# Score rows fetched through ScalarE's DMA queue, and the loads of x handed out one by one

## The chip, the cores and the metric

The kernel runs on one core of a Trainium2 chip. The core has five engines that run their own instruction streams and meet through semaphores: TensorE (PE, matmuls into PSUM; its weight loads are shown as PEld), VectorE (DVE), ScalarE (ACT), GpSimd (POOL) and SyncE (SP), which in this kernel only issues DMA transfers. The metric is the device time of one execution in microseconds.

## The reference, cut to what matters

```python
# attention with mixed heads: B=8 batches, H=12 heads, S=448 rows, D=64
scores = scale * q @ k^T                       # per head
scores = einsum('bhij,hg->bgij', scores, w_pre)   # heads mixed before the softmax
attn   = softmax(scores)
attn   = einsum('bhij,hg->bgij', attn, w_post)    # and again after it
x      = (attn @ v) as [B*S, H*D] = [3584, 768]
# dense part
out    = ((x @ w1) * (x @ w2)) @ w3 @ w_out       # 768 -> 1024 -> 1024 -> 768
```

Everything is float32. The weights w3 and w_out are multiplied with each other once, so the dense part is two products in, one product out.

## The kernel before, in words

**Attention.** Heads can only be mixed when the twelve heads of a score row lie on the partition axis. So the scores of a batch are made per pair of heads on TensorE (`qk`, line 175), copied out of PSUM by ScalarE (lines 180 and 181) and stored to DRAM (`raw_d`, lines 186 and 189). From there they are read back in another layout by `fetch` (line 196): ten rows of a batch times twelve heads make a block, two blocks make a **set**, and there are 180 sets. A set's tile `r` has two buffers. Its fetch is two DMAs (line 203), or four where a set crosses the end of a batch (line 210). Then, for set m:

- `mix(m)` on TensorE (line 221) multiplies `r` with w_pre into PSUM banks 2 and 3;
- `largest(m)` on VectorE (line 228) reduces the row minimum (the sign was turned), `exp(m)` on ScalarE (line 236) reads the two banks, so `mix(m+1)` can only start when `exp(m)` has read them;
- `scale(m)` on VectorE and GpSimd (lines 245 to 248) makes the scaled w_post;
- `post(m)` on TensorE (line 261) mixes again, ScalarE copies the result to `mt` (line 275);
- `av` (line 302) multiplies with v, once for fifteen blocks.

**Dense part.** Matmuls are done in three products of split float32 (high and low parts). The first two batches (`ONE = 2`) go one by one with x in SBUF. The other six go in three pairs; a pair's four quarters of x (called 11, 21, 12, 22, three tiles each) are combined in a scheme of seven products instead of eight. Each of the seven products of a layer is a **phase** (`phases`, `layer`): a list of loads (of quarters of x from DRAM), a list of preparations (VectorE sums, a ScalarE cast to the high part at line 641, a GpSimd difference for the low part at line 642) and groups of matmuls (line 703). A phase has 36 matmuls ("atoms"). The loads of a phase are asked for two phases ahead and the preparations are made one phase ahead. The weights of a group, a unit `wu`, are loaded by line 394 into a ring of buffers, three or four units ahead.

**The order of the work** is written out by hand in `run` (from line 891). The loop has 366 steps; set m owns the steps 2m and 2m+1. An even step 2m does: `fetch(m+2)` first (lines 927 and 928); then the stores and loads that the step before put on a list (`do_later`: weight loads, stores, then the loads of x, in this order); `largest(m)`; a share of dense atoms; `exp(m)`; more atoms. An odd step does `scale(m)`, atoms, `av` where it is due, `post(m-1)`, `mix(m+1)`, and the `qk` of later batches with its two copies by ScalarE. Every engine gets its instructions in this order. A wait of one instruction holds up whatever stands behind it on the same engine.

**DMA.** All 1292 transfers are issued by SyncE, in program order. `LATE` (line 34) is step 107, at which buffers of the first phase of the program are given back. `PAIR` is the step at which the pairs begin; `pair_setup` (line 717) issues the first pair's loads of x.

Of the kernel before, what the change touches and what calls it, by code (L numbers as in the profile page):

```python
# [15 lines left out]
B, H, S, D = 8, 12, 448, 64  # L16
# [8 lines left out]
KF, K1 = FF // 128, DM // 128  # L25
IH = IB // 2
HK = H * IH
PP = 64
# [5 lines left out]
LATE = 2 * NB + GB + 2  # L34
# [16 lines left out]
class Kernel:  # L51
# [144 lines left out]
    def fetch(self, m):  # L196
        r = self.rp.tile([128, 2, S], F32, tag="r", name=f"r{m}", bufs=2)
        self.rs[m] = r
        b, t = divmod(2 * m, NB)
        if t + 1 < NB and self.width(2 * m + 1) == IB:  # L200
            src = self.raw_d[b][t * IB:(t + 2) * IB].rearrange("(c s i) h j -> s (i h) c j", c=2, s=2)
            for s in range(2):
                self.nc.sync.dma_start(r[s * PP:s * PP + HK], src[s])
            return
        for c in range(2):
            b, t = divmod(2 * m + c, NB)
            for s in range(2):
                k = self.half(2 * m + c, s)
                src = self.raw_d[b][t * IB + s * IH:t * IB + s * IH + k].rearrange("i h j -> (i h) j")
                self.nc.sync.dma_start(r[s * PP:s * PP + H * k, c], src)  # L210

    def half(self, n, s):
        return min(IH, self.width(n) - s * IH)
# [392 lines left out]
    def layer(self, name, b, nk, pair, groups, h):  # L606

        nc = self.nc
        acc = {g: {} for g in groups}
        ops = {}  # L610
        t2 = [None] * nk
        order, loads = (ORDER3, {}) if b else (ORDER1, {1: (11, 21), 2: (12, 22)})

        def load(q):
            half, batch = q // 20, 2 * pair + (q % 10 == 2)
            assert self.x_made[batch] == 2 * NG
            b[q] = [self.take(f"x{name}_{q}_{k}") for k in range(nk)]
            for k in range(nk):
                nc.sync.dma_start(b[q][k], self.x_d[batch][half][:, k])

        def sub(out, x, y):
            nc.vector.tensor_tensor(out, x, y, op=ALU.subtract)

        def t1(k):
            sub(b[12][k], b[12][k], b[11][k])

        def prepare(m, k):
            x, last = {1: (11, False), 2: (21, False), 3: (22, True), 5: (12, True), 7: (11, True)}.get(m, (0, m == 4))
            x = b[x][k] if x else t2[k]
            if m == 6:  # L630
                x = t2[k] = self.take(f"t{name}_{k}")
                sub(x, b[22][k], b[12][k])
            elif m == 7:
                sub(x, t2[k], x)
            elif m == 4:
                sub(x, b[21][k], x)
                self.give(b[21][k])

            def split():
                hi, lo = (self.take(f"{p}{name}_{m}_{k}", F32R) for p in ("eh", "el"))  # L640
                nc.scalar.copy(hi, x)  # L641
                nc.gpsimd.tensor_tensor(lo, x, hi.bitcast(F32), op=ALU.subtract)  # L642
                ops[m, k] = hi, lo
                if last:
                    self.give(x)

            self.soon.append((None, split))

        def gather(m, g, p):

            a = acc[g]

            def put(out, *to):
                if out not in a:
                    a[out] = self.take(f"c{name}_{g[0]}_{g[1]}_{out}")
                if to:
                    nc.vector.tensor_tensor(a[out], a[to[0]], p, op=ALU.add)  # L657
                else:
                    nc.scalar.copy(a[out], p)

            if m == 1:
                put(11 if order == ORDER3 else 12)
            elif m == 2:
                put(11, 11 if order == ORDER3 else 12)
                ready(g, 11)
            elif m == 6:
                put(12, 11 if order == ORDER3 else 12)
            elif m == 7:
                put(21, 12)
            elif m == 5:  # L670
                put(22, 21)
                put(12, 12)
                ready(g, 22)
            else:
                q = {3: 12, 4: 21}[m]
                put(q, q)
                ready(g, q)

        def ready(g, q):
            f, w = g  # L680
            if w == 1:
                def mult():
                    x, y = acc[f, 0][q], acc[f, 1][q]
                    nc.gpsimd.tensor_tensor(x, x, y, op=ALU.mult)
                    self.give(y)
                    h[q][f] = x
                self.soon.append((None, mult))
            elif w == 3:
                d, batch = f + (q // 20) * K1 // 2, 2 * pair + (q % 10 == 2)
                dst, x = self.out[d * 128:(d + 1) * 128, batch * S:(batch + 1) * S], acc[g][q]  # L690

                def store():
                    nc.sync.dma_start(dst, x)
                    self.give(x)
                self.later.append(store)

        def group(m, g):
            w = self.next_unit()
            i = self.next_bank()
            p = self.bank(i, f"e{name}_{m}_{g[0]}_{g[1]}")[:, :S]  # L700
            for k in range(nk):
                for t, (x, y) in enumerate(PAIRS):
                    nc.tensor.matmul(p, w[:, k, x], ops[m, k][y],  # L703
                                     start=(k == 0 and t == 0), stop=(k == nk - 1 and t == 2))
                    yield
            if g == groups[-1]:
                for k in range(nk):
                    self.give(*ops.pop((m, k)))
            self.ends.append((i, lambda: gather(m, g, p)))

        early = order[order.index(6) - 1]
        for m in order:
            jobs = [lambda k=k: t1(k) for k in range(nk)] if m == early else []
            yield ([lambda q=q: load(q) for q in loads.get(m, ())],
                   [lambda k=k, m=m: prepare(m, k) for k in range(nk)] + jobs, [group(m, g) for g in groups])

    def pair_setup(self, phases):
# [7 lines left out]
    def pair_experts(self, phases):  # L725

        for i, (_, _, groups) in enumerate(phases):
            todo = [f for x in phases[i + 2:i + 3] for f in x[0]]
            todo = [lambda f=f: self.x_due.append(f) for f in todo]
            todo += [f for x in phases[i + 1:i + 2] for f in x[1]]  # L730
            n, each = 0, min(6, 30 // len(todo)) if todo else 1
            for g in groups:
                for _ in g:
                    if n % each == 0 and todo:
                        todo.pop(0)()
                    n += 1
                    yield
            assert not todo
# [315 lines left out]
```

## Time and profile before

| | |
|---|---|
| median of three runs | 1438.72 us (1436.74 to 1440.12) |
| profiled execution, its own time | 1439.32 us |
| its span, first to last instruction | 1437.5 us, mean granted TensorE clock 0.989 |
| busy: PE / PEld / DVE / ACT / POOL | 1382.0 / 1053.5 / 741.6 / 832.5 / 619.8 us |
| DMA moved | 416.87 MB, 290 GB/s on average |

How to read it. A matmul's start is measured and its end is modelled; neighbouring matmuls overlap, so a row's duration is longer than the distance to the next one. An idle time is put down to what ended it. A DMA-issuing instruction is not counted as busy; on the timeline it has the time that its engine's sequencer needed to issue it, and its transfer lands some microseconds later. "SPq" is SyncE's sequencer. Times on the timeline are from the start of the span; set 54, the first that the change touches, is mixed at about 394 us, and the last set at about 1241 us. After that only the dense part of the last pair remains.

### The profile page before, as it was taken

The page shows a single profiled execution, that of the slowest core. Times are in us where ns is not written, and L with a number is a line of the kernel's source. Part 1 is how long each engine was busy: PE and PEld are TensorE (multiplying, and loading weights), DVE is VectorE, ACT ScalarE, POOL GpSimd, SP SyncE. Part 2 cuts the span into 40 slices and gives each one's busy share as a digit, 9 for nine tenths or more (in the row PEclk, how much of TensorE's full clock was granted, in tenths as well). Part 3 has the DMA queues.
Part 4 walks back from the last instruction along what each step waited for, and adds up shares of the span by engine and source line. Part 5 has one row for each costly group of instructions (what it writes and reads, how often), then busy time and mean ns, then how long its engine had stood idle before and what let it go on. Part 6 is the DMA issues. An engine that isn't in the chain of part 4 may idle for free.

```text
span 1437.5 us, 45779 instructions
## 1 busy us (share of the span) xinstructions
PE 1382.0 (96%) x18684; PEld 1053.5 (73%) x18684; DVE 741.6 (52%) x1497; ACT 832.5 (58%) x1952; POOL 619.8 (43%) x754
## 2 busy tenths in 40 slices
PE   5779999999999999999999999999999999999998
PEld 2357786776677667776777777777777777899988
DVE  6867567667544545432444436333445446345563
ACT  4867666777766656665656557556555445432231
POOL 2433233434433544532345336334335446446693
PEclk8989999999999999999999999999999999999999
DMA  9998789999989999999989978799879757698775
GB/s 294 368 330 274 241 271 314 318 312 312 330 281 348 350 363 318 373 357 338 289 268 295 320 259 280 249 318 350 285 223 297 239 176 224 195 337 270 230 232 172
DMA packets 203761, 416.87 MB, mean 290 GB/s; under 512 B 20528, under 2 KB 120112, under 8 KB 203472
## 3 DMA queue, kind: packets, MB, share of 16 engines
q1 hardware_dynamic: 203552, 413.94, 87.4%
q8 instruction: 149, 2.44, 0.7%
q14 instruction: 60, 0.49, 0.1%
HBM read 279.77 MB, written 134.09 MB: 288 GB/s over the span
## 4 chain that ended last, share of the span: by engine, by line
PE 80%; DMA 11%; DVE 4%; ACT 2%; issue 1%; POOL 1%; SPq 0%; DVEq 0%; POOLq 0%; ACTq 0%
PE e L703 20%; PE psa L302 11%; PE pso L261 10%; PE psm L221 8%; PE psq L175 7%; PE eg L523 5%; PE psf L361 4%; PE eo L554 4%; PE e2o L703 4%; PE e3o L703 4%; PE e1o L703 3%; DMA wu<-w_d 3%; DMA raw_d<-st 2%; DMA r<-raw_d 2%; DMA x<-x_d 1%
## 5 line engine op out<-in xcount | busy, mean ns | idle before, releaser
L248 POOL TENSOR_SCALAR w<-wpo,ri 128x60 f32<-128x60 f32 x360 | 180.4, 517 | 487.1 <-DVE ri L246 467.8
L228 DVE TENSOR_REDUCE mn<-psm 128x1 f32<-128x448 f32 x360 | 207.6, 618 | 322.5 <-PE psm L221 322.2
L275 ACT COPY mt<-pso 128x480 f32<-128x480 f32 x352 | 197.9, 621 | 184.5 <-PE pso L261 184.3
L703 PE MATMUL e<-eh,wu 128*128 128x448 f32 x1008 | 296.7, 371 | 5.3 <-DVE c L657 3.2
L236 ACT ACTIVATE e<-psm,mn 128x448 f32<-128x448 f32 x360 | 226.8, 642 | 7.9 <-DVE mn L228 7.9
L703 PEld LDWEIGHTS e<-eh,wu 128*128 128x128 f32 x1008 | 187.5, 188 | 50.9 <-issue 25.7
L221 PE MATMUL psm<-r,wsc 60*64 60x448 f32 (+1 forms) x1440 | 194.0, 552 | 21.1 <-DVE cx L125 8.3
L261 PEld LDWEIGHTS pso<-w,e 60*64 60x64 f32 x10080 | 174.7, 134 | 50.7 <-issue 42.5
L261 PE MATMUL pso<-w,e 60*64 60x60 f32 x10080 | 198.5, 224 | 0.4 <-ACT mt L275 0.3
L703 PE MATMUL e<-el,wu 128*128 128x448 f32 x504 | 186.9, 371 | 0.0
L302 PE MATMUL psa<-mt,v 128*64 128x150 f32 (+1 forms) x2304 | 156.9, 292 | 3.2 <-ACT st L180 3.2
L175 PE MATMUL psq<-kq 64*64 64x448 f32 x1176 | 156.4, 542 | 3.4 <-ACT st L180 3.4
L302 PEld LDWEIGHTS psa<-mt,v 128*64 128x64 f32 x2304 | 143.6, 137 | 19.3 <-ACT st L180 5.9
L657 DVE TENSOR_TENSOR c<-c,e 128x448 f32<-128x448 f32 x168 | 101.6, 617 | 87.5 <-PE e L703 82.9
L180 ACT COPY st<-psq 128x448 f32<-128x448 f32 x162 | 86.4, 533 | 77.1 <-ACT mt L275 33.5
L523 PE MATMUL eg<-xh,wu 128*128 128x448 f32 x384 | 119.1, 380 | 4.8 <-DMA wu<-w_d 4.8
L642 POOL TENSOR_TENSOR el<-x,eh 128x448 fp32r<-128x448 f32 x90 | 103.8, 1173 | 31.8 <-ACT eh L641 26.2
L703 PEld LDWEIGHTS e<-el,wu 128*128 128x128 f32 x504 | 94.6, 188 | 22.6 <-issue 14.1
L175 PEld LDWEIGHTS psq<-kq 64*64 64x64 f32 x1176 | 61.2, 135 | 57.7 <-issue 29.7
L523 PEld LDWEIGHTS eg<-xh,wu 128*128 128x128 f32 x384 | 71.4, 189 | 37.5 <-issue 24.0
L245 DVE TENSOR_SCALAR sa<-sm 128x2 f32<-128x2 f32 x180 | 35.5, 197 | 115.1 <-ACT e L236 114.6
L181 ACT COPY st<-psq 128x448 f32<-128x448 f32 x162 | 87.6, 541 | 0.0
(99 smaller groups left out, 2007.5 us busy)
## 6 DMA issues: line engine op xcount, KB each, us to landing
r<-raw_d SPq DMA_DIRECT2D x344, 210.0 KB, 5.0
raw_d<-st SPq DMA_DIRECT2D x138, 448.0 KB, 5.7
wu<-w_d SPq DMA_DIRECT2D x104, 384.0 KB, 6.6
wu<-s_d SPq DMA_DIRECT2D x96, 384.0 KB, 4.9
wu<-w_d SPq DMA_DIRECT2D x51, 512.0 KB, 5.7
kq<-kq SPq DMA_DIRECT2D x42, 448.0 KB, 7.4
wu<-s_d SPq DMA_DIRECT2D x36, 512.0 KB, 5.1
x<-x_d SPq DMA_DIRECT2D x72, 224.0 KB, 5.8
```

The lines of the kernel that those rows point to most:

```text
L175: nc.tensor.matmul(ps[s][z * PP:(z + 1) * PP], t[rows, q:q + PP], t[rows, k:k + S], start=True, stop=True)
L221: nc.tensor.matmul(ps[s][c * PP:(c + 1) * PP, :S], self.wsc[k], r[k, c], start=True, stop=True)
L228: self.nc.vector.tensor_reduce(mn[:, s:s + 1], self.psm[m][s][:, :S], axis=AX.X, op=ALU.min)
L236: nc.scalar.activation(e, p[:, :S], AF.Exp, bias=mn[:, s:s + 1], scale=-1.0, accum_out=sm[:, s:s + 1])
L248: nc.gpsimd.tensor_scalar_mul(w2[:, s], self.wpo, ri[:, s:s + 1])
L261: nc.tensor.matmul(self.pso[c][z * PP:(z + 1) * PP, at:at + HK], e[k, j * PP:(j + 1) * PP], w2s[k, s], start=True, stop=True)
L275: self.nc.scalar.copy(dst.rearrange("p j g (s i) -> p j s g i", s=2), src)
L302: nc.tensor.matmul(self.psa[rows, g % 3, :W], v[:, j, rows], mt[:, j, 2 * g + s, :W], start=(j == 0), stop=(j == NJ - 1))
L523: nc.tensor.matmul(p, u[:, k % (K1 // 2), x], xs[y][:, k], start=(k == 0 and t == 0), stop=(k == K1 - 1 and t == 2))
L642: nc.gpsimd.tensor_tensor(lo, x, hi.bitcast(F32), op=ALU.subtract)
L657: nc.vector.tensor_tensor(a[out], a[to[0]], p, op=ALU.add)
L703: nc.tensor.matmul(p, w[:, k, x], ops[m, k][y], start=(k == 0 and t == 0), stop=(k == nk - 1 and t == 2))
```

## The change

Two edits. In `fetch`, the DMAs of sets whose first block has a number of at least 107 (sets 54 to 179) are issued by ScalarE instead of SyncE, at the same place of the program order: at the head of the even step, ahead of the step's other instructions. ScalarE has a DMA queue of its own. In the pairs, a load of a quarter of x, until now one job that issues its three tiles, becomes three jobs of one tile each. These jobs alternate with the preparations of the phase, a preparation first, and are called every three atoms; before, the two quarters' jobs came first, at atoms 0 and 6, and the preparations followed every six atoms. This touches ten phases, those two phases ahead of a layer's first and second product; the loads that `pair_setup` issues stay as they are.

```diff
     def fetch(self, m):
...
+        dma = self.nc.scalar.dma_start if 2 * m >= LATE else self.nc.sync.dma_start
...
-                self.nc.sync.dma_start(r[s * PP:s * PP + HK], src[s])
+                dma(r[s * PP:s * PP + HK], src[s])
...
-                self.nc.sync.dma_start(r[s * PP:s * PP + H * k, c], src)
+                dma(r[s * PP:s * PP + H * k, c], src)
...
-        def load(q):
+        def load(q, only=None):
...
-            b[q] = [self.take(f"x{name}_{q}_{k}") for k in range(nk)]
-            for k in range(nk):
+            b[q] = b.get(q, [None] * nk)
+            for k in range(nk) if only is None else (only,):
+                b[q][k] = self.take(f"x{name}_{q}_{k}")
                 nc.sync.dma_start(b[q][k], self.x_d[batch][half][:, k])
...
-            yield ([lambda q=q: load(q) for q in loads.get(m, ())],
+            yield ([lambda only=None, q=q: load(q, only) for q in loads.get(m, ())],
...
-            todo = [f for x in phases[i + 2:i + 3] for f in x[0]]
-            todo = [lambda f=f: self.x_due.append(f) for f in todo]
-            todo += [f for x in phases[i + 1:i + 2] for f in x[1]]
-            n, each = 0, min(6, 30 // len(todo)) if todo else 1
+            loads = [f for x in phases[i + 2:i + 3] for f in x[0]]
+            loads = [lambda f=f, k=k: self.x_due.append(lambda: f(k)) for f in loads for k in range(K1 // 2)]
+            made = [f for x in phases[i + 1:i + 2] for f in x[1]]
+            todo = [f for x in itertools.zip_longest(made, loads) for f in x if f]
+            n, each = 0, min(6, max(30, 3 * K1 // 2 * len(groups) - 16) // len(todo)) if todo else 1
```

## The prediction

> **What bounds the kernel now.** I read the head of the page, then TensorE's waits from 380 us on, where the changed part begins, then SyncE's waits, the table by stage, and last the timelines of the places where TensorE stood still.
>
> ```profile
> span 1437.5 us, 45779 instructions
> ...
> PE 1382.0 (96%) x18684; PEld 1053.5 (73%) x18684; DVE 741.6 (52%) x1497; ACT 832.5 (58%) x1952; POOL 619.8 (43%) x754
> ```
>
> ```profile
> PE eg L523 <- DMA wu<-w_d: 4.8, 4, 1.8
> PE psm L221 <- DMA r<-raw_d: 3.4, 2, 2.0
> ...
> PE e L703 <- DMA wu<-w_d: 1.4, 1, 1.4
> ```
>
> TensorE is the bound. From 380 us on it waits for transfers seven times, 9.6 us in all: that is the most the change can win, 0.7%. These waits have their place, as three stages of the table by stage show (the columns are the stretch and its length, the granted clock, the DMA engines' busy share, GB/s):
>
> ```profile
> 475.00:530.00 55.00, 0.94 1.03 364
> 960.00:1010.00 50.00, 1.00 1.04 348
> 700.00:760.00 60.00, 1.00 0.81 253
> ```
>
> The first two hold most of the waits, and there all sixteen DMA engines are full (share 1.0); the third is a quiet stage with 0.81. In full stages a transfer is late because the DMA engines are behind, whoever issues it.
>
> SyncE's own longest wait is the fetch, which stands at the head of the even step and cannot start before the mix that last read its buffer:
>
> ```profile
> SPq L203 <- PE psm L221: 243.4, 81, 6.2
> ```
>
> So in quiet stages the fetch holds up what is queued behind it on SyncE, 3.0 us at a time (243.4 / 81). In the full stages something else holds it. The chain of waits there, and SyncE's queue in order:
>
> ```profile
> 986.43 7.07 DMA x<-x_d
> ...
> 993.57 6.28 DMA r<-raw_d
> ```
>
> ```profile
> 986.43 2.62 SPq L619 DMA_DIRECT2D x<-x_d  x3
> 989.75 0.32 SPq L394 DMA_DIRECT2D wu<-w_d  x1
> 990.23 0.34 SPq L693 DMA_DIRECT2D out<-c1o  x1
> 991.16 2.19 SPq L619 DMA_DIRECT2D x<-x_d  x3
> 993.57 0.88 SPq L203 DMA_DIRECT2D r<-raw_d  x2
> ```
>
> The fetch at 993.57 is issued when the x load of 986.43 has landed (986.43 + 7.07 = 993.50), and that load stands eight places ahead of it: 3 + 1 + 1 + 3. Eight transfers are in flight and the ninth waits for the oldest. I take it that this count goes by program order over both queues. **This is the point on which the forecast rests:** then a fetch on ScalarE waits for the same old transfer, and ScalarE stands still meanwhile, where until now only SyncE did.
>
> **The fetch, part by part.** Removed from SyncE and added to ScalarE: sets 54 to 179, 120 with two DMAs and 6 with four, 264 issues.
>
> ```profile
> L203 SPq DMA_DIRECT2D r<-raw_d x344: 315/392/1914, 14.9 to 1224.7; - x172
> ```
>
> ```profile
> L236 ACT ACTIVATE e<-psm,mn 128x448 f32<-128x448 f32 x256 | 161.6, 644 | 5.0 <-DVE mn L228 5.0
> L275 ACT COPY mt<-pso 128x480 f32<-128x480 f32 x251 | 141.1, 621 | 160.2 <-PE pso L261 160.1
> ```
>
> ```profile
> 988.59 0.54 ACT L181 COPY st<-psq 128x448 f32<-128x448 f32 x1
> 989.01 0.58 ACT L641 CAST eh<-x 128x448 fp32r<-128x448 f32 x1
> 989.48 0.65 ACT L236 ACTIVATE e<-psm,mn 128x448 f32<-128x448 f32 x1
> ```
>
> At the median of 0.392 us on SyncE that is 103 us of ScalarE's sequencer, 0.8 us per set in front of `exp`. ScalarE's instructions overlap (the cast starts 0.12 us before the copy has ended), so its sequencer runs ahead of the engine, and the two copies of `st` that stand before the fetch can cover the issue. Bounds: 0 (all covered) to 0.8 us per set. I take it as covered: even uncovered it ends in ScalarE's 160 us of waiting for `post`. Without that cover it lands on `exp`, and behind `exp` on the next mix, which needs the banks that `exp` reads; that is a rival below.
>
> **The new wait.** Queued behind a waiting fetch are the casts of the step, `exp`, then the copies; TensorE's next mix waits for `exp`. For each late fetch: how far its end lies behind the start of the first ScalarE instruction after it; that delay moves the end of `exp` (two of 0.644, so 1.28 after its start); what lies beyond the start of the next mix is a stall.
>
> ```profile
> 473.69 1.15 ACT L484 CAST s<-y 128x512 fp32r<-128x512 f32 x2
> 475.16 0.66 ACT L236 ACTIVATE e<-psm,mn 128x448 f32<-128x448 f32 x1
> 475.45 0.88 SPq L203 DMA_DIRECT2D r<-raw_d  x2
> 476.61 0.54 PE L221 MATMUL psm<-r,wsc 60*64 60x448 f32 x1
> ...
> 513.74 0.52 ACT L484 CAST s<-y 128x384 fp32r<-128x384 f32 x1
> 514.22 0.64 ACT L236 ACTIVATE e<-psm,mn 128x448 f32<-128x448 f32 x1
> 516.84 1.18 SPq L203 DMA_DIRECT2D r<-raw_d  x2
> 517.14 0.54 PE L221 MATMUL psm<-r,wsc 60*64 60x448 f32 x1
> ...
> 586.20 0.65 ACT L236 ACTIVATE e<-psm,mn 128x448 f32<-128x448 f32 x1
> 586.77 1.19 SPq L203 DMA_DIRECT2D r<-raw_d  x2
> 588.48 0.54 PE L221 MATMUL psm<-r,wsc 60*64 60x448 f32 x1
> ...
> 663.24 1.84 ACT L641 CAST eh<-x 128x448 fp32r<-128x448 f32 x3
> 664.99 0.63 ACT L236 ACTIVATE e<-psm,mn 128x448 f32<-128x448 f32 x1
> 666.96 1.55 SPq L203 DMA_DIRECT2D r<-raw_d  x2
> 665.93 0.54 PE L221 MATMUL psm<-r,wsc 60*64 60x448 f32 x1
> ...
> 992.32 0.54 PE L221 MATMUL psm<-r,wsc 60*64 60x448 f32 x1
> ```
>
> - At 475: fetch ends 476.33, delay 2.64, `exp` ends 476.44 + 2.64 = 479.08, mix at 476.61: 2.5. SyncE may have come late here for reasons of its own, so 2.0.
> - At 517: fetch ends 518.02, delay 4.28, `exp` 515.50 + 4.28 = 519.78, mix at 517.14: 2.6.
> - At 587: fetch ends 587.96; a cast of about 0.4 stands between; `exp` from 588.4 to 589.7, mix at 588.48: 1.2.
> - At 667: fetch ends 668.51, delay 5.27, `exp` 666.27 + 5.27 = 671.54, mix at 665.93: 5.6. Its two issues took 1.55 against a median of 0.78; with that 0.77 off, 4.8.
> - At 993: fetch ends 994.45, delay 5.44, `exp` 990.76 + 5.44 = 996.20, mix at 992.32: 3.9.
>
> Together 14.5 us. A neighbouring late fetch adds nothing: TensorE then stands still while the DMA engines catch up. For the same reason the old waits in these places go: 4.8 for weights and 3.4 for r, 8.2. The net is +6.3. Bounds: half the new wait, if fewer transfers are in the way, 7.2 - 8.2 = -1.0; nothing replaced, +14.5.
>
> **What SyncE gains.** The 243 us of waiting no longer stand in front of weights and loads. I take 0: these waits end in quiet stages, where TensorE does not wait for transfers. Bounds: 0 to the 1.4 us of `wu` at 1100 that the sum has not used.
>
> **The loads of x.** Sixty tile loads in ten phases stay on SyncE, same issues, later by up to 24 - 6 = 18 atoms; of six, one comes in the first step of the phase, then two, then three, so they still come bunched. The DMA engines have the same bytes to move in the full stage around 990: 0. Preparations come 12 atoms earlier and have a phase of room before the matmuls read them: 0. The first load now has 33 atoms until its cast:
>
> ```profile
> 727.36 3.85 PE e L703 x18
> ```
>
> ```profile
> DMA to landing us min/median/max: 4.6/5.8/8.6
> ```
>
> 33 x 3.85 / 18 = 7.1 us of dense matmuls alone, with attention in between, against 8.6 at worst for landing (the view of line 619). Bounds: 0 to about 1.5 us each for the few that fall in a full stage, +3; I take 0.
>
> **Sum.** The profiled execution took 1439.3 us, 1.8 more than its span and 0.6 more than the median of 1438.7. 1439.3 + 6.3 - 0.6 = **1445 us**.
>
> The Trainium skill has two rules that bear on this. "DMA: Bandwidth & Descriptors", section "Issuing engines are not separate DMA queues": transfers from several issuing engines share the same sixteen DMA engines, and a second issuer only saves issue time; the full stages here agree (share 1.03 and 1.04), and by it the fetch lands no sooner. The same page, "Queues, rings and completion order": each DMA engine takes turns between the queues that have work, packet by packet; by it the fetch would pass what is queued on SyncE's ring. No run here has two queues yet, and the sum above is the same by both, since the wait lies before the issue.
>
> **Rivals.**
>
> - *SyncE's freedom wins.* With no fetch in front, weights go out 3 us sooner before each full stage, the eight places are free when ScalarE comes, and the old waits go: 9.6 us at most, so 1429; with half the r waits left, about 1432. For it: the 243.4 us. Against: the full stages are 35 to 55 us long, and nothing can be moved out of them by 3 us. By the skill's rule of shared engines the r waits of 3.4 stay and it would be 1438.7 - 6.2 = 1432.5; by the rule of taking turns they go and it is 1429.
> - *The two cancel.* The fetches are themselves among the eight and land sooner on a ring of their own, so that ScalarE waits half as long: 7.2 new against 8.2 old, 1438.
> - *Issue on ScalarE costs more.* If it is not covered, or takes longer than on SyncE, it decides where `exp` ends less than 0.8 us before the next mix, which is before about 690 us (at 475 above: 476.44 against 476.61). Forty-odd sets at 0.2 more each: 9 us on top, 1454.
>
> **How the numbers follow.** The forecast has 0.47 with its own range 1442 to 1450; costly issue 0.12; cancelling 0.21; freedom 0.20. What this kernel's measurement can tell from no change is about 0.2%, 2.9 us. Slower: 0.47 + 0.12, less a little of the forecast's low end, 0.57; the same 0.23; faster 0.20. The range 1432 to 1454 leaves about a tenth out on each side.
>
> **What would show it.** In ScalarE's sequencer waits of the fetch by DMAs, several us long near 475, 517, 667 and 990; in TensorE's waits a line of `psm` on ScalarE's `e` of some 10 to 15 us from 380 us on, and those on `r` and `wu` smaller. SyncE's wait at line 203 for `psm` falls to the first 53 sets. If `psm` on `e` stays below 3 us, my reading of the eight places is wrong; if it is spread over many sets, it is the issue time.

## The result, and the profile after

The changed kernel takes 1452.04 us (median of six runs, 1446.64 to 1456.34) against 1440.36 us for the kernel before on the same chip (1436.74 to 1442.04, six runs). The ratio is 1.0088, with a 95% interval of 1.0066 to 1.011. So it is 11.7 us slower, where 6.3 were forecast. Run again beside other kernels it took 1449.3 us against 1439.2, a ratio of 1.0082 (1.0052 to 1.0111). The profiled execution took 1446.7 us, span 1445.0, which is 7.4 us over the profiled one of before. It was one of the two fastest of the six. The new lines of the kernel shift its line numbers by one from line 199 on, and by two behind the load of x.

The head of the page after, and its queues (packets, megabytes, share of the sixteen engines' time):

```profile
span 1445.0 us, 45817 instructions
...
PE 1387.5 (96%) x18684; PEld 1055.8 (73%) x18684; DVE 745.3 (52%) x1497; ACT 840.0 (58%) x1952; POOL 624.7 (43%) x754
...
q1 hardware_dynamic: 169514, 359.99, 73.5%
q10 hardware_dynamic: 34038, 53.95, 13.1%
```

Queue q10 is ScalarE's and new; it carries the fetches. TensorE does the same matmuls and is still the bound. Its waits after, from 380 us on, all of them (total, times, longest):

```profile
PE psm L222 <- ACT e L237: 13.0, 11, 3.0
PE e L705 <- DVE c L659: 2.6, 3, 1.5
PE e L705 <- ACT eos L562: 0.9, 1, 0.9
PE e L705 <- ACT c L661: 0.2, 1, 0.2
```

The names: `psm` is the mix, `e` in front of L237 the result of `exp`; `eos` and `c` are ScalarE's and VectorE's copies and sums of the dense part's results, `eg` (below) its matmuls in the first two batches. One of the eleven waits of `psm` for `e`, 0.44 us at 380 us, lies ahead of the first fetch on ScalarE (387.7 us), and the kernel before has it as well, at 378.9 us (from its waits between 370 and 385 us):

```profile
PE psm L221 <- ACT e L236: 0.4, 1, 0.4
```

Apart from that one there were, before, 9.6 us of waits for weights and for r, and none of `psm` for `e`. After, every wait for a transfer is gone, and 12.5 us of the mix waiting for `exp`, in ten places, have come. In sum TensorE waits 16.3 us in place of 13.4.

The largest of these stalls shows how it comes about. First TensorE, then ScalarE with its queue, then SyncE's queue; each row has its start, its length, and in brackets the idle time before it with what ended it:

```profile
521.22 1.08 PE L262 MATMUL pso<-w,e 60*64 60x60 f32 x56
525.28 2.38 PE L222 MATMUL psm<-r,wsc 60*64 60x448 f32 x8 [2.98 <-ACT e L237]
```

```profile
518.15 1.14 ACT L276 COPY mt<-pso 128x480 f32<-128x480 f32 x2
521.94 2.06 ACTq L204 DMA_DIRECT2D r<-raw_d  x2
524.09 0.51 ACT L485 CAST s<-y 128x384 fp32r<-128x384 f32 x1 [4.81 <-DMA raw_d<-st]
524.51 0.63 ACT L237 ACTIVATE e<-psm,mn 128x448 f32<-128x448 f32 x1
```

```profile
516.36 1.30 SPq L186 DMA_DIRECT2D raw_d<-st  x2
518.58 0.33 SPq L395 DMA_DIRECT2D wu<-w_d  x1
520.03 0.33 SPq L488 DMA_DIRECT2D s_d<-s  x1
522.42 0.32 SPq L395 DMA_DIRECT2D wu<-w_d  x1
523.16 0.32 SPq L488 DMA_DIRECT2D s_d<-s  x1
523.58 0.37 SPq L395 DMA_DIRECT2D wu<-w_d  x1
```

ScalarE's two fetch issues take 2.06 us, because the second waits. What ends the wait is a store of raw scores, which has nothing to do with these rows: it writes another batch. Counted back in program order over both queues it stands eight places ahead: two stores, `wu`, `s_d`, `wu`, `s_d`, `wu`, and the set's own first fetch. By the trace's DMA records that store landed at 523.65 us, and the second fetch was issued at 523.67. The first fetch had waited too: the transfer eight places ahead of it, the second one of the set before, landed at 521.84 us, and it was issued at 521.94. The records also show what the eight are. The transfers of both queues tell of their landing through the same eight semaphores (100 to 104 and 106 to 108), handed out in turn; the store and the second fetch both have 106. ScalarE did nothing for 4.81 us, `exp` began at 524.51, and the mix behind it stood for 2.98 us. In the whole trace at least 18 of the 264 fetch issues (of some predecessors the landing is not recorded) were made within 0.1 us of the landing of the transfer eight places ahead, at 431 to 496, 524 to 541, 620 to 691, 786 to 792, 1005 and 1102 to 1107 us.

The waits do not show the whole price. The groups of the two matmul lines that use ScalarE's results, from 380 us on, before and after:

```profile
L221 PE MATMUL psm<-r,wsc 60*64 60x448 f32 x1030 | 130.3, 544 | 3.5 <-DMA r<-raw_d 3.4
L175 PE MATMUL psq<-kq 64*64 64x448 f32 x776 | 98.1, 535 | 0.0
```

```profile
L222 PE MATMUL psm<-r,wsc 60*64 60x448 f32 (+1 forms) x1032 | 136.2, 545 | 13.0 <-ACT e L237 13.0
L175 PE MATMUL psq<-kq 64*64 64x448 f32 x776 | 102.4, 539 | 0.0
```

The busy time of the mix has grown by 5.9 us and that of `psq` by 4.3, with the same instructions. A mix writes two banks. When the first `exp` has freed its bank, TensorE starts, and then stands again until the second `exp`, 0.6 us later, frees the other. That second stop lies between matmuls of one group, where ends are modelled, so the trace counts it as busy. It shows in the starts: in the set that stalls at 1007.8 us the first and the last of the eight matmuls start 1.1 us apart, in an undisturbed set (two are shown below) 0.4 to 0.5.

```profile
L222 PE MATMUL psm<-r,wsc x8: 536/562/587, 1007.8 to 1008.9; 60*64 60x448 f32 x8
```

In all ten sets with a stall the distance is larger, in nine by that 0.6 us and in one, at half clock, by 1.0. The `psq` that follow begin within the same stop, so the 5.9 and the 4.3 us are in part the same time.

With two issues a set, the issue itself costs nothing that shows. On ScalarE one takes less than on SyncE (0.392 us before):

```profile
L204 ACTq DMA_DIRECT2D r<-raw_d x240: 322/323/1856, 387.7 to 1232.4; - x120
```

And through the quiet stage the two kernels keep step. The mixes of sets 120 and 140 (eight matmuls each; shortest, median and longest in ns, start of the first and of the last), before and after:

```profile
L221 PE MATMUL psm<-r,wsc x8: 536/539/542, 837.9 to 838.4; 60*64 60x448 f32 x8
...
L221 PE MATMUL psm<-r,wsc x8: 536/539/542, 980.0 to 980.4; 60*64 60x448 f32 x8
```

```profile
L222 PE MATMUL psm<-r,wsc x8: 536/539/542, 844.8 to 845.2; 60*64 60x448 f32 x8
...
L222 PE MATMUL psm<-r,wsc x8: 536/539/542, 987.1 to 987.5; 60*64 60x448 f32 x8
```

That is 142.1 us for twenty sets before and 142.3 after. By the starts of the mixes, the changed kernel falls back in the full stages: by 2.3 us between sets 60 and 72, 5.7 between 80 and 96 and 1.1 between 140 and 144. Between 96 and 112 it makes up 2.4.

### The profile page after: what moved, and what is told of

It is laid out like the page before. It is cut to its first block, busy times and chain, and to the rows that moved or that the text cites. A ratio compares the mean times of both kernels' runs of the same rounds, so it can differ in the third digit from the quotient of the medians.

```text
span 1445.0 us, 45817 instructions
## 1 busy us (share of the span) xinstructions
PE 1387.5 (96%) x18684; PEld 1055.8 (73%) x18684; DVE 745.3 (52%) x1497; ACT 840.0 (58%) x1952; POOL 624.7 (43%) x754
## 4 chain that ended last, share of the span: by engine, by line
PE 47%; DMA 4%; DVE 1%; ACT 1%; issue 0%; ACTq 0%; POOL 0%; SPq 0%; DVEq 0%; POOLq 0%
PE e L705 20%; PE psa L303 5%; PE pso L262 5%; PE psm L222 4%; PE e2o L705 4%; PE e3o L705 4%; PE e1o L705 3%; DMA x<-x_d 2%; PE psq L175 2%; DMA wu<-w_d 1%; ACT e L237 0%; DMA v<-v 0%; DMA r<-raw_d 0%; DVE c L659 0%; DVE c L624 0%
## 5 line engine op out<-in xcount | busy, mean ns | idle before, releaser
L237 ACT ACTIVATE e<-psm,mn 128x448 f32<-128x448 f32 x360 | 225.2, 633 | 46.0 <-DVE mn L229 9.8
L222 PE MATMUL psm<-r,wsc 60*64 60x448 f32 (+1 forms) x1440 | 198.2, 552 | 30.1 <-ACT e L237 19.8
L175 PE MATMUL psq<-kq 64*64 64x448 f32 x1176 | 159.8, 541 | 4.7 <-ACT st L180 4.7
```

Source lines behind the costliest of these rows:

```text
L175: nc.tensor.matmul(ps[s][z * PP:(z + 1) * PP], t[rows, q:q + PP], t[rows, k:k + S], start=True, stop=True)
L222: nc.tensor.matmul(ps[s][c * PP:(c + 1) * PP, :S], self.wsc[k], r[k, c], start=True, stop=True)
L237: nc.scalar.activation(e, p[:, :S], AF.Exp, bias=mn[:, s:s + 1], scale=-1.0, accum_out=sm[:, s:s + 1])
```

## The experiments

Theory: a fetch on ScalarE waits for the transfer eight places ahead and holds `exp`, and with it the mix. Rivals: the loads of x; the issue itself; the second queue; SyncE's order.

**Half of the change: the fetch alone**

```diff
+        dma = self.nc.scalar.dma_start if 2 * m >= LATE else self.nc.sync.dma_start
...
-                self.nc.sync.dma_start(r[s * PP:s * PP + HK], src[s])
+                dma(r[s * PP:s * PP + HK], src[s])
...
-                self.nc.sync.dma_start(r[s * PP:s * PP + H * k, c], src)
+                dma(r[s * PP:s * PP + H * k, c], src)
```

> Half of the change alone: ScalarE issues the score rows from set 54 on, the pairs' loads of x stay as before in jobs of three tiles. Theory (a fetch that waits for an old transfer holds up exp, and exp the next mix): nearly the whole loss is here, 6 to 12 us above the kernel before, and TensorE's wait of psm for e from 380 us on is again 10 to 15 us (13.0 with both halves). Rival (the spread loads of x cost half of it, through ScalarE's 16.7 us of waiting for x): no more than half, 3 to 6 us above.

Measured: 1454.47 us (1449.82 to 1461.73), ratio 1.011 (1.0077 to 1.0143), 14.6 us slower. The whole loss is here, and more than the range I gave. `psm` on `e` was 7.0 us only, below the 10 to 15 expected; other instructions of ScalarE were held in its place:

```profile
775.05 1.05 ACTq L211 DMA_DIRECT2D r<-raw_d  x2
775.43 0.54 ACT L181 COPY st<-psq 128x448 f32<-128x448 f32 x1
776.40 2.52 ACTq L211 DMA_DIRECT2D r<-raw_d  x2
778.96 0.56 ACT L642 CAST eh<-t 128x448 fp32r<-128x448 f32 x1 [2.99 <-DMA wu<-w_d]
```

This is set 112, whose rows lie in two batches and need four transfers. The last two issues waited for a weight load, and behind them stood a cast that TensorE then waited for (1.62 us at 778). The prediction had counted six such sets, and gave them no cost of their own.

**The other half: the loads of x alone**

```diff
-        dma = self.nc.scalar.dma_start if 2 * m >= LATE else self.nc.sync.dma_start
+        dma = self.nc.sync.dma_start
```

> The other half alone: the pairs' loads of x go out one tile at a time between preparations, the score rows stay with SyncE. Theory: within 2 us of the kernel before, up to 2 us slower, psm never waits for e longer than 1 us in all beyond the kernel before. Rival (the spread loads are half of the loss): 4 to 6 us slower, with casts that wait for x.

Measured: 1437.04 us (twelve runs, 1433.95 to 1441.68) against 1439.87 (23 runs), ratio 0.9978 (0.9961 to 0.9994). Neither the theory nor the rival: it is 2.8 us faster, little more than can be told from no change. TensorE's first three waits, from 380 us on:

```profile
PE eg L524 <- DMA wu<-w_d: 3.4, 3, 2.1
PE e L705 <- DVE c L659: 3.2, 5, 1.5
PE psm L222 <- DMA r<-raw_d: 2.3, 1, 2.3
```

The wait for r of 1.5 us at 998 us, which was in the profile of before, is not there. SyncE's queue at that place now has the x loads in ones and twos between weights and stores, so fewer of them stand right ahead of a fetch. One profile of each doesn't show that this is the whole gain. ScalarE's casts did wait for x here, 13.9 us in all (0.7 before, 16.7 in the changed kernel), and it cost nothing that the time shows. So these waits alone aren't the loss.

**The fetch on ScalarE, but behind exp**

```diff
-            if not odd and LF <= n + LF < N:
+            if not odd and LF <= n + LF < N and n + LF < LATE:
                 self.fetch(m + LF // 2)
...
             if not odd and m < SETS:
                 self.exp(m)
+            if not odd and LATE <= n + LF < N:
+                self.fetch(m + LF // 2)
```

> The changed kernel, but from set 54 on ScalarE issues the fetch after the two exp of the even step instead of ahead of them; queue, count and addresses as in the changed kernel. Theory (the wait in front of exp is the loss): psm's wait for e from 380 us on falls from 13.0 to under 4 us, the time falls by 4 to 9 us against the changed kernel, to 1443 to 1448; something of it comes back as waits for r, since the rows are asked for half a step later. Rival (ScalarE's issue time, or the second queue's use of the DMA engines, is the loss wherever the issue stands): within 2 us of the changed kernel's 1452.

Measured: 1444.56 us (twelve runs, 1436.88 to 1450.92), ratio 1.0032 (1.0011 to 1.0053). That is 7.5 us less than the changed kernel's 1452.04, and 4.7 less than the 1449.3 of its later runs. From the waits, 380 us on, of an execution of 1446.86 us:

```profile
PE psm L222 <- DMA r<-raw_d: 3.7, 6, 1.3
PE e L705 <- ACT eos L562: 3.4, 1, 3.4
...
PE psm L222 <- ACT e L237: 0.4, 1, 0.4
```

Queue, count and bytes are the same. What stands behind a waiting fetch has changed, and with the fetch's place in the program order also which transfer is eight ahead of it. ScalarE still stands behind fetches, for up to 4.6 us, but now in front of the copies `mt` and `eos`. `psm` on `e` falls from 13.0 to 0.4 us, as the theory says, and those 0.4 us lie at 380 us, ahead of the change. So more than half of the loss is not the second queue's. A loss of some 4.7 us is left; in the profile the copies `eos` and `c` are now late (3.4 and 2.4 us), and the rows come a little late.

**SyncE's fetch behind the step's other transfers**, the same edit in the kernel before:

```diff
-            if not odd and LF <= n + LF < N:
+            if not odd and LF <= n + LF < N and n + LF < LATE:
                 self.fetch(m + LF // 2)
...
             if not odd and m < SETS:
                 self.exp(m)
+            if not odd and LATE <= n + LF < N:
+                self.fetch(m + LF // 2)
```

> The kernel before, but from set 54 on SyncE issues the fetch later in the even step, behind the step's stores, weights and loads of x, so that it no longer stands in front of them; ScalarE issues nothing. Theory (SyncE's 243 us of waiting for psm hide in quiet stages and are worth nothing): within 3 us of the kernel before, with more waiting for r in the full stages and less for weights. Rival (SyncE's freedom is worth something, and the change only lost it again on ScalarE): 3 to 8 us faster than before.

Measured: 1455.23 us, ratio 1.0111 (1.0074 to 1.0147). 15.4 us slower, though ScalarE issues nothing; neither the theory nor the rival had that. TensorE's wait for r and SyncE's longest wait:

```profile
PE psm L221 <- DMA r<-raw_d: 10.7, 7, 3.3
```

```profile
SPq L189 <- ACT st L181: 152.6, 59, 4.6
```

SyncE's wait of 243.4 us for `psm` is not saved. Most of it moves to the stores, which wait for ScalarE's copies (17.8 us before), and the fetch then stands behind these and comes late. So in this kernel, on SyncE, its place at the head of the step is worth 15 us.

**Twice as many issues on ScalarE**

```diff
             for s in range(2):
-                dma(r[s * PP:s * PP + HK], src[s])
+                for i in range(2 if 2 * m >= LATE else 1):
+                    p = slice(30 * i, 30 * i + 30) if 2 * m >= LATE else slice(0, HK)
+                    dma(r[s * PP + p.start:s * PP + p.stop], src[s][p])
```

> The changed kernel, but each of ScalarE's two fetch transfers of a set is issued as two of half the rows: four issues a set instead of two, the same bytes, the same place. Theory (the fetch waits for the transfer eight places ahead, in the full stages): the third and fourth issue wait for younger transfers, so psm's wait for e from 380 us on grows from 13 to 20 us or more, all of it in the full stages at 430 to 690 and near 1000 and 1100, and the time by 5 to 20 us over the changed kernel. Rival (the issue itself costs ScalarE): 126 sets at 2 more issues of 0.32 us, some 80 us if they are not covered, spread over all stages, the quiet ones between sets 112 and 140 too.

Measured: 1524.08 us (four runs), ratio 1.0582 (1.0541 to 1.0623), 72 us over the changed kernel. That is far over the 5 to 20 that the theory gave, and near the rival's 80. The profiled execution was the slowest of the four (1534.13).

```profile
PE psm L224 <- ACT e L239: 38.6, 20, 5.7
```

```profile
r<-raw_d ACTq DMA_DIRECT2D x498, 105.0 KB, 4.4
```

The transfers, now half as large, are no slower (4.4 us to landing, 4.8 in the changed kernel). In the quiet stage between sets 118 and 136 a set takes 0.24 us more than before (128.75 against 124.37 us for 18). Over all 126 sets that would be some 31 us: an estimate of the part that doesn't depend on the stage. It need not be issue time alone, since ScalarE stands behind a waiting fetch there too, once for 2.4 us. The rest stands in the full stages: the lag behind the kernel before grows by 23 us between sets 56 and 72, by 27 between 80 and 96, and by 13 between 136 and 144. So both have a share once a set has four issues, and the one in the full stages is the larger.

**ScalarE's fetch only from the pairs on**

```diff
-        dma = self.nc.scalar.dma_start if 2 * m >= LATE else self.nc.sync.dma_start
+        dma = self.nc.scalar.dma_start if 2 * m >= 4 * NB + 11 else self.nc.sync.dma_start
```

> The changed kernel, but ScalarE issues the fetch only from the pairs on (set 96 and after); before that SyncE does. Theory: the loss goes with the full stages, of which all but those near 1000 and 1100 lie before the pairs: 1439 to 1444, psm's wait for e at most 5 us from 380 us on. Rival (every fetch on ScalarE costs the same): two thirds of the 126 sets remain, so two thirds of the loss, about 1448.

Measured: 1447.96 us (1446.47 to 1456.34), ratio 1.0077 (1.0047 to 1.0107). I had the place wrong: the time is the rival's, and `psm` waits 8.7 us for `e`, not at most 5. But the loss isn't paid evenly, as the rival has it. Of the 7 us that the profile lies behind from set 88 to the end, five come between sets 88 and 96, where the pairs begin and their loads of x go out together, and none between sets 120 and 140; three more come up to set 112, and one is made up at the end. The place:

```profile
668.00 1.01 ACTq L204 DMA_DIRECT2D r<-raw_d  x2
669.13 1.50 ACT L643 CAST eh<-x 128x448 fp32r<-128x448 f32 x3 [3.84 <-DMA x<-x_d]
670.53 0.62 ACT L237 ACTIVATE e<-psm,mn 128x448 f32<-128x448 f32 x1
```

```profile
671.30 1.21 PE L222 MATMUL psm<-r,wsc 60*64 60x448 f32 x5 [3.21 <-ACT e L237]
```

Three casts stand between the late fetch and `exp` and add 1.4 us to its delay.

**The fetch on GpSimd**

```diff
-        dma = self.nc.scalar.dma_start if 2 * m >= LATE else self.nc.sync.dma_start
+        dma = self.nc.gpsimd.dma_start if 2 * m >= LATE else self.nc.sync.dma_start
```

> The changed kernel, but GpSimd issues the fetch from set 54 on, at the same place in the order; loads of x spread as in the changed kernel. Theory (what costs is that ScalarE stands in front of exp while the fetch waits): psm's wait for e is under 2 us from 380 us on; GpSimd stands still instead, whose products of the weights w2 and whose el come later. If its waits are as long as ScalarE's and its work has room, the time is that of the spread loads alone, 1435 to 1442; if TensorE then waits for w2 or el as it did for e, 1445 to 1455. Rival (a second queue beside SyncE's slows the transfers whoever issues it): 1448 to 1456, with waits for wu or r.

Measured: 1437.52 us (twelve runs), ratio 0.9994 (0.9975 to 1.0013): as the loads of x alone (1437.04). TensorE's wait of `psm` for `e`, what GpSimd does for its fetches, and SyncE's longest wait:

```profile
PE psm L222 <- ACT e L237: 0.9, 1, 0.9
```

```profile
L204 POOL DMA_DIRECT2D r<-raw_d x240: 634/666/900, 385.5 to 1223.6; - x120
```

```profile
SPq L189 <- ACT st L181: 187.3, 63, 5.4
```

Here SyncE is as free of the fetch as in the changed kernel, ScalarE never stands behind a fetch, and nothing is won. The mix and `psq` are back at 129.9 and 98.8 us. Two things changed at once: the engine that stands is another, and by the DMA records GpSimd's transfers use eight semaphores of their own (111 to 118), so its fetches aren't among the eight. This run alone doesn't part the two. The one with the fetch behind `exp` does so for more than half of the loss: there the two queues shared the eight as in the changed kernel.

**The changed kernel once more**

> The changed kernel once more, beside the others on this chip. Expected 1450 to 1454 as a median. Theory on the clock: TensorE runs at a granted clock of 0.5 for some 3 or 7 us behind a pause of two microseconds or more, so an execution with two or three such pauses in the changed part is 2 to 7 us longer than its waits say. Rival: the spread between executions has nothing to do with the pauses, and the stretches of low clock stand elsewhere.

Measured: 1449.3 us (1445.69 to 1455.91), a little below the 1450 to 1454 expected; profiled span 1447.2 us, `psm` on `e` 11.0 us. Its two stretches of low clock stand behind pauses of 2.2 us at 521 and 2.0 at 672, as the theory on the clock has it (a third pause, 1.7 us at 1008, has none behind it), and the last section shows more; how much of the spread between executions it makes remains open.

## Why the prediction was right, and where its sizes were off

**The point on which the forecast rested** held: eight transfers in flight, counted in program order over both queues, and a fetch on ScalarE that stands until the eighth ahead has landed. The 0.02 us between landing and issue shows it, and moving the fetch behind `exp` shows that more than half of the loss arises there.

**The new wait**, 14.5 us in five places, was 12.5 in ten. But the sum counted each stall to the end of the second `exp`, and the profile's wait ends with the first. With the second stop of 0.6 us for each set, the stalls are 2.0 us at 475 (given as 2.0), 1.5 and 3.6 at 517 (2.6), 1.5 at 593 (1.2 at 587), 2.7 at 674 (4.8 at 667) and 2.5 at 1006 (3.9 at 993). The two that were given as largest were little more than half of that. A neighbouring late fetch was to add nothing, and at 517 two sets in a row stalled. Stalls of 0.8 to 1.6 us at 434, 623, 781 and 1098 us were not foreseen.

**The old waits** were to fall by 8.2; all 9.6 went, and with them some 2.4 us of second stops behind late rows in the kernel before (sets 69, 96 to 99 and 143).

**The terms that were mis-sized** are these two: the stalls, 18.6 us in place of 14.5, and what they replace, 12.0 in place of 8.2. The net by this count is +6.6 against the +6.3 of the sum, because the two errors cancel; that is luck. Between the two profiles 6.0 of the 7.4 us come after 380 us; 1.4 had come before the first changed instruction. In these 6.0 us TensorE's waits account for 16.3 - 13.4 = 2.9, and 3.1 are growth of its busy time, in which the second stops lie. The clock works against them: the kernel before has a stretch of half clock (last section) that took 3.4 us of full clock, the changed kernel's took 1.7, which is also why `eg` fell from 66.9 to 64.7 us. These parts don't add up closer than to a microsecond or two. The distance from 7.4 to the median's 11.7 lies between executions: the profiled one had a granted clock of 0.990, the five others 0.982 to 0.986. That clock doesn't order them strictly (1446.64 us at 0.985), so where these 4.3 us come from stays open.

**Issue time, taken as covered,** was: nothing in the quiet stage. The rival that made it 9 us falls. What neither had is the sets with four transfers. In the fetch alone set 112 paid, and not because an issue is long: the last two of the four waited for a weight load. That four take half of the eight places is the likely reason; no run varies it by itself.

**The rival that the two cancel** falls as well. The fetches land hardly sooner on their own queue (median 4.8 us, before 4.9 over the same stretch), and the new waits are 12.5, not 7.2.

**SyncE's freedom, taken as 0,** was 0 within what the runs can tell, and the rival falls: with GpSimd as the issuer SyncE is free, nobody pays for it, and the time is that of the loads of x alone. The Trainium skill, "DMA: Bandwidth & Descriptors", section "Issuing engines are not separate DMA queues", says that a second issuer saves only the time to initiate a transfer. These runs agree (1437.5 us with GpSimd, 1437.0 without a second issuer). They show besides that the new issuer pays for the waiting: ScalarE stood 4.81 us behind the fetch of one set.

**The loads of x, taken as 0 with a bound of +3,** were -2.8 (ratio 0.9978). The sign of the bound was wrong; that spread loads leave fewer transfers ahead of a fetch is the likely reason. That the two edits together lie 2.4 us (1452.04) below the fetch alone (1454.47) fits, but those intervals overlap.

The fastest kernel of the study is the loads of x alone, 1437.0 us. It lies below both the kernel before and the changed one, and level with the fetch on GpSimd.

## What to carry to other kernels

A transfer moved to a compute engine takes its waits with it. Before moving one, count which transfer it will wait for, and read what stands behind it on the new engine in the place where the DMA engines are full, before what its issue takes. If it must move, put it behind the instruction that others wait for, or on an engine that has room, as GpSimd had here. And one that the next step needs early belongs at the head of its queue: SyncE's long wait there was not a cost.

## What the hardware showed that was not expected

**Short pauses of TensorE are often followed by a stretch at half its clock.** The granted clock is the share of TensorE's full clock that the chip gave it. The columns are the stretch and its length, busy times and counts of PE, PEld, DVE, ACT and POOL, granted clock, DMA share, GB/s. The kernel before, behind a pause of 1.75 us for weights:

```profile
521.03 0.47 PE L523 MATMUL eg<-xh,wu 128*128 128x448 f32 x1 [1.75 <-DMA wu<-w_d]
```

```profile
522.00:529.00 7.00, 6.06 (x73) 3.95 (x75) 2.09 (x4) 1.12 (x2) 2.73 (x3) 0.52 1.04 374
```

In these seven microseconds 7 x (1 - 0.52) = 3.4 us of full clock are lost, nearly twice the pause. The changed kernel, behind a pause of 2.06 us at 673.80, loses nothing:

```profile
676.00:683.00 7.00, 7.00 (x99) 4.50 (x100) 2.62 (x8) 4.66 (x12) 3.29 (x6) 1.00 1.05 378
```

In all ten profiles, from 380 us to the last matmul, every stretch of low clock stood at or right behind a pause or a pair of pauses of 1.6 to 5.8 us in all, and took away 1.7 or 3.4 us of full clock, in one place 5.1. Of the pauses in that range some were followed by none, such as the 3.21 us at 668 us in the run with ScalarE's fetch from the pairs on. The Trainium skill, "TensorE: Matmul & The Clock Gate", section "HAM oscillation — how this bites in real kernels", puts the rule at no idle gaps over about 3.4 us. Here 1.75 us was enough in one execution, and 3.21 not in another, so the rows don't bear out a fixed length of that size. With the clock that goes with it, a pause can so cost 1.4 to three times its length, and which pause it is differs between executions of one kernel: in the changed kernel a pause of 2.0 us at 672 us had such a stretch behind it when it was run again, and the one of 2.06 us above had none.

**Issuing a transfer from GpSimd is work of that engine.** The profile counts the 0.666 us of each issue as its busy time (619.8 us before, 793.7 with its fetches), and in the trace hardly any of it overlaps GpSimd's other instructions: 2.5 us over 264 issues. ScalarE's 0.323 us run on its sequencer beside the engine: of the 118 us that its 264 issues took, 75 overlap ScalarE's other instructions. In this kernel GpSimd had the room.
